# Group 3's keys and queries transposed by the DMA crossbar, through the buffer that the later groups share

## The chip, the cores and the metric

The kernel runs on one core of one Trainium2 chip. Its time is device microseconds (us) from launch to end, the median of several executions. The engines are named as in the profile: PE (TensorE, matrix multiply; PEld is its weight load, which overlaps), DVE (VectorE), ACT (ScalarE), POOL (GpSimd) and SP (SyncE). In this kernel POOL does almost nothing but issue the loads from HBM that also convert float32 to bf16. SP issues the DMA transposes and the stores of the output. SPq and POOLq are the rows of these two queues in the profile.

## What is computed

Windowed attention with a few "sink" positions, and behind it a SwiGLU block. Cut to what matters:

```python
# q, k, v: [4, 8, 768, 64] float32; n_sink = 4; window = 128
scores = (q @ k.transpose(0, 1, 3, 2)) / sqrt(64)
keep   = (pos_k < n_sink) | ((0 <= pos_q - pos_k) & (pos_q - pos_k < window))
a      = softmax(where(keep, scores, -1e9))
x      = (a @ v).transpose(0, 2, 1, 3).reshape(3072, 512)      # heads side by side

g      = x @ w_gate                                            # [3072, 1536]
out    = (g * sigmoid(g) * (x @ w_val)) @ w_out                # [3072, 512]
```

The kernel cuts the 3072 tokens into 12 attention groups of 256 tokens, three to each of the 4 batches: groups 0 to 2 belong to batch 0, groups 3 to 5 to batch 1, and so on. The SwiGLU block works in token blocks of 256, 256, 256, 512, 512, 512, 512 and 256. PE runs the SwiGLU matmuls nearly without a break, and the attention of later groups is woven in between them.

## The kernel before: the parts concerned

The scores need keys and queries with the head dimension on the partitions, but they come from HBM with the tokens there. So each group's k and q are loaded into a tile `nat` and transposed into `kT` and `qT`, 128 tokens at a time. There are two ways to do it. `step_TN` uses PE (a transpose into PSUM, then a copy by ACT or DVE). `xbar` uses DMA transposes on the SP queue, which go from on-chip memory to on-chip memory and use no compute engine.

```python
    rowp = pool("rowp", 3)
    natp = pool("natp", 1)               # one buffer
    kqtp = pool("kqtp", 2)
    ...
    def load_nat(g):
        b, c = divmod(g, GC)
        x = (natp if g > 3 else rowp).tile(
            [P, 2, 2, DM], BF16, tag="nat" if g > 3 else "rows", name="nat")
        for i, src in ((0, k), (1, q)):
            for j in range(2):           # four loads: k j0, k j1, q j0, q j1
                t0 = c * 256 + j * P
                nc.gpsimd.dma_start(
                    x[:, i, j].rearrange("p (h d) -> p h d", d=D),
                    src[b, :, t0:t0 + P].rearrange("h p d -> p h d"))
        nats[g] = x
    ...
    def step_TN(g, i, j, evict="av"):    # by PE: 4 transposes, one copy
        ...
        pt = bank([P, NP2, P], BF16, "pn")
        for p in range(NP2):
            nc.tensor.transpose(pt[:, p], nats[g][:, i, j, p * P:(p + 1) * P], ident)
        t0 = c * 256 + j * P
        dst = (kTs, qTs)[i][b][:, :, t0:t0 + P]
        if evict[i] == "a":
            nc.scalar.copy(out=dst, in_=pt)
        else:
            nc.vector.tensor_copy(out=dst, in_=pt)

    def xbar(g):                         # by DMA: k j0, q j0, k j1, q j1
        ...
        for j in range(2):
            for i in range(2):
                t0 = c * 256 + j * P
                nc.sync.dma_start_transpose(
                    (kTs, qTs)[i][b][:, :, t0:t0 + P], nats[g][:, i, j])
    ...
    def NV(g):                           # the loads of k, q and then v of a group
        return L(A(load_nat, g), A(load_v, g))
```

`step_S` computes a group's scores, in two halves of four heads. Each half needs all of the group's 256 keys and queries, and the 128 keys ahead of them if the group isn't the first of its batch. `step_K` does the scores of the sink keys. `step_PV` multiplies the weights by v, and `step_X` transposes the result into `xT` for the SwiGLU matmuls: by PE for groups 0, 1, 2 and 4, and by DMA transposes on the SP queue for the others. `gate` is one unit of the SwiGLU's first half, `down` is one of its second half, and `weave` puts attention steps into numbered units. Units 0 to 17 of the first weave are `gate`, units 18 to 23 are `down`:

```python
    ... # prologue: groups 0 and 1; POOL has issued the weights and the loads of groups 1 and 2
    load_nat(3)
    load_v(3)
    ...
    weave(us, slots(
        ...
        ((4, 4, 5, 5), TN(2)), ((6, 7), Ss(2)), (6, [K(2)]),
        ...
        (11, [NV(4)]), ((14, 14, 15, 15), TN(3, "aa")),
        (15, [A(xbar, 4)]), (15, [NV(5)]), (19, [A(xbar, 5)]), (19, [NV(6)]),
        (23, [A(xbar, 6)]), (23, [NV(7)]),
        ((17, 18), Ss(3)), (18, [A(step_ks, 1)]), (18, [A(step_vsb, 1)]),
        ((19, 19, 19, 20), PVs(3)), (20, Xs(3)),
        ((19, 20), Ss(4)), (19, [K(4)]),
        ((21, 21, 22, 22), PVs(4)), (22, Xs(4))))

    weave(gates(3) + downs(3), slots(...))   # its first unit needs all of xT of groups 3 and 4
```

The order in which the program names the steps is the order on each engine's queue. POOL issues loads one after another and waits at the first one whose buffer isn't free. SP does the same with transposes and stores. `natp` has one buffer, so a load of `nat` into it waits until the four transposes of the group before have read it. In the kernel before, group 4 is its first user.

Of the kernel before, what the change touches and what calls it, by code (L numbers as in the profile page):

```python
# [8 lines left out]
BF16 = mybir.dt.bfloat16  # L9
# [5 lines left out]
def kernel(  # L15
# [13 lines left out]
    P = 128  # L29
# [3 lines left out]
    DM = moe_w_gate.shape[0]  # L33
# [19 lines left out]
    def pool(name, bufs, psum=False):  # L53
        if psum:
            return ctx.enter_context(
                tc.tile_pool(name=name, bufs=bufs, space=bass.MemoryType.PSUM))
        return ctx.enter_context(tc.tile_pool(name=name, bufs=bufs))
# [3 lines left out]
    rowp = pool("rowp", 3)  # L61
    natp = pool("natp", 1)
# [15 lines left out]
    def bank(shape, dtype, name):  # L78
        return psum.tile(shape, dtype, tag="b", name=name)


    rows, nats, vas = {}, {}, {}
# [20 lines left out]

    def load_nat(g):
        b, c = divmod(g, GC)
        x = (natp if g > 3 else rowp).tile(
            [P, 2, 2, DM], BF16, tag="nat" if g > 3 else "rows", name="nat")
        for i, src in ((0, k), (1, q)):
            for j in range(2):
                t0 = c * 256 + j * P  # L110
# [4 lines that stand above are left out]
# [81 lines left out]
    load_gate(2)  # L196
    nc.gpsimd.tensor_copy(out=vcf[64:128], in_=vcf[0:64])
    load_nat(2)
    load_gate(3)
    load_v(2)  # L200
# [27 lines left out]
    def new_T(b):  # L228
        if b not in kTs:
            kTs[b] = kqtp.tile([P, NP2, S], BF16, tag="kT", name="kT")  # L230
            qTs[b] = kqtp.tile([P, NP2, S], BF16, tag="qT", name="qT")
# [17 lines left out]
        else:  # L249
            nc.vector.tensor_copy(out=dst, in_=pt)  # L250

    def step_TN(g, i, j, evict="av"):

        b, c = divmod(g, GC)
        new_T(b)
        pt = bank([P, NP2, P], BF16, "pn")
        for p in range(NP2):
            nc.tensor.transpose(pt[:, p], nats[g][:, i, j, p * P:(p + 1) * P], ident)  # L258
        t0 = c * 256 + j * P
        dst = (kTs, qTs)[i][b][:, :, t0:t0 + P]  # L260
        if evict[i] == "a":
            nc.scalar.copy(out=dst, in_=pt)
        else:
            nc.vector.tensor_copy(out=dst, in_=pt)
# [219 lines left out]
    def A(fn, *a):  # L484
        return lambda: fn(*a)

    def TN(g, evict="av"):
        return [A(step_TN, g, i, j, evict) for j in range(2) for i in range(2)]

    def Ss(g):  # L490
        return [A(step_S, g, p2) for p2 in range(2)]
# [108 lines left out]
    later[:0] = masks1  # L600
    flush()
    load_nat(3)
    load_v(3)

# [5 lines left out]
    def L(*fs):  # L610
        def f():
            for x in fs:
                x()
        return f

    def NV(g):
        return L(A(load_nat, g), A(load_v, g))

    weave(us, slots(
        (0, [K(1)]), (1, PVs(1)[:2] + [A(step_PV, 1, 0, 1, "a"), A(step_PV, 1, 1, 1, "a"), flush]),  # L620
        (2, [A(step_X, 1, 0, "a"), A(step_X, 1, 1, "a")]),
        ((4, 4, 5, 5), TN(2)), ((6, 7), Ss(2)), (6, [K(2)]),
        ((8, 8), PVs(2)[:2]), (9, [A(step_PV, 2, 0, 1, "a"), A(step_PV, 2, 1, 1, "a")]),
        ((10, 11), [A(step_X, 2, 0, "a"), A(step_X, 2, 1, "a")]),
        (11, [NV(4)]), ((14, 14, 15, 15), TN(3, "aa")),
        (15, [A(xbar, 4)]), (15, [NV(5)]), (19, [A(xbar, 5)]), (19, [NV(6)]),
        (23, [A(xbar, 6)]), (23, [NV(7)]),
        ((17, 18), Ss(3)), (18, [A(step_ks, 1)]), (18, [A(step_vsb, 1)]),
# [59 lines left out]
```

## Time and profile before

| what | value |
|---|---|
| time, median of 3 | 241.11 us (240.41 to 241.32) |
| span of the profiled execution | 238.4 us |
| PE busy | 229.5 us, 96% of the span, 1928 instructions |
| DVE busy | 157.8 us, 66% |
| ACT busy | 114.8 us, 48% |
| POOL busy | 73.2 us, 31% |
| DMA transposes from `nat` | 32: 16 into `kT`, 16 into `qT` |
| PE transposes from `nat` (groups 2 and 3) | 32 of 219 ns each, at 26.2 to 50.8 us |

A page of the profile lists busy time by engine, the chain of work that ended last (followed back from the last instruction, each step to what released it), and the costliest groups of instructions. The trace behind it can be asked for a timeline of one engine: start, duration, what it did, and in square brackets how long the engine had been idle and what ended that. For a DMA, the timeline shows when its engine issued it. When its data landed is given separately, as microseconds from issue to landing. A transposing DMA has no landing time of its own, so it is read from who was waiting for it.

### The profile page before, as it was taken

The numbers are of one execution on the slowest core, as the hardware profiler recorded it, in microseconds if no ns is written. First come the engines' busy times: TensorE is split into PE (matmuls) and PEld (weight loads), VectorE is DVE, ScalarE is ACT, GpSimd is POOL, SyncE is SP. The second block draws the span as 40 slices with busy tenths as digits, with TensorE's granted clock in tenths as the row PEclk, the third lists the DMA queues.
The fourth block names the chain that finished last, engine by engine and source line by source line (L and its number), as shares of the span: only waits on it lengthen the run. The fifth ranks groups of instructions, "written<-read, shape, count | busy, mean of one in ns | idle before, by whom it ended". The sixth has DMA issues, their size and how long they took to land.

```text
span 238.4 us, 4972 instructions
## 1 busy us (share of the span) xinstructions
PE 229.5 (96%) x1928; PEld 132.7 (56%) x1952; DVE 157.8 (66%) x336; ACT 114.8 (48%) x237; POOL 73.2 (31%) x94
## 2 busy tenths in 40 slices
PE   7898999999999999999999999999999999999994
PEld 4567978895554444444445454444454445488443
DVE  5698778768652898950798970688960598877000
ACT  4796485467452835512845622655622653333222
POOL 8985964703517053160171700071000000000000
PEclk9999999999999999999999999999999999999999
DMA  7999999993999979799599955799505100200122
GB/s 128 174 184 177 181 201 203 156 138 68 161 168 174 158 113 138 105 131 199 114 111 128 130 32 159 101 109 141 69 0 161 62 0 3 44 0 3 68 109 88
DMA packets 107591, 27.36 MB, mean 115 GB/s; under 512 B 94640, under 2 KB 104624, under 8 KB 107568
## 3 DMA queue, kind: packets, MB, share of 16 engines
q0 software_dynamic: 76640, 13.90, 74.1%
q1 hardware_dynamic: 30400, 12.89, 27.8%
q8 instruction: 15, 0.25, 0.4%
q10 hardware_dynamic: 528, 0.26, 0.4%
q14 instruction: 8, 0.07, 0.1%
HBM read 28.34 MB, written 6.29 MB: 145 GB/s over the span
## 4 chain that ended last, share of the span: by engine, by line
PE 85%; DMA 6%; DVE 4%; issue 2%; ACT 1%; POOL 1%; POOLq 0%; DVEq 0%; ACTq 0%
PE pd L467 26%; PE pv L436 24%; PE pg L436 24%; DMA wv<-in_moe_w_val_dram 4%; PE s L305 4%; PE o L368 4%; DMA x<-in_q_dram 2%; PE pt L243 1%; DVE u L449 1%; PE pn L258 1%; DVE xn L382 1%; DVE ht L450 1%; PE pk L333 1%; PE o L348 1%; DVE e L317 1%
## 5 line engine op out<-in xcount | busy, mean ns | idle before, releaser
L436 PE MATMUL pv<-xT,wv 128*128 128x256 bf16 (+1 forms) x376 | 73.6, 325 | 1.2 <-DMA wv<-in_moe_w_val_dram 0.5
L436 PE MATMUL pg<-xT,wg 128*128 128x256 bf16 (+1 forms) x377 | 73.5, 325 | 0.7
L443 ACT ACTIVATE th<-pg 128x512 f32<-128x512 f32 x72 | 43.4, 603 | 62.2 <-PE pg L436 58.3
L449 DVE SCALAR_TENSOR_TENSOR u<-th,pg 128x512 bf16<-128x512 f32 x72 | 49.1, 682 | 35.8 <-ACT th L443 35.8
L467 PE MATMUL pd<-wo,ht 128*128 128x512 bf16 (+1 forms) x291 | 65.0, 370 | 0.4
L450 DVE TENSOR_TENSOR ht<-u,pv 128x512 bf16<-128x512 bf16 x72 | 49.5, 687 | 11.5 <-PE pv L436 5.1
L436 PEld LDWEIGHTS <-wg 128*128 128x128 bf16 x384 | 37.4, 98 | 26.2 <-issue 0.9
L436 PEld LDWEIGHTS <-wv 128*128 128x128 bf16 x384 | 34.3, 97 | 20.4 <-issue 1.7
L312 ACT ACTIVATE e<-s 128x512 bf16<-128x512 f32 (+1 forms) x88 | 42.7, 580 | 3.9 <-PE s L305 3.9
L467 PEld LDWEIGHTS <-ht 128*128 128x128 bf16 x300 | 28.1, 98 | 28.7 <-issue 0.5
L111 POOL DMA_DIRECT2D nat<-in_k_dram x20 | 17.6, 883 | 80.2 <-DMA qT<-nat 68.2
L471 ACT ACTIVATE ot<-pd 128x512 f32<-128x512 f32 (+1 forms) x25 | 14.6, 583 | 48.4 <-PE pd L467 46.4
L317 DVE TENSOR_TENSOR e<-e,mask 128x1024 bf16<-128x1024 bf16 (+1 forms) x44 | 26.9, 648 | 3.6 <-ACT e L312 3.6
L122 POOL DMA_DIRECT2D va<-in_v_dram x24 | 21.4, 908 | 4.8 <-DMA wo<-in_moe_w_out_dram 2.5
L368 PEld LDWEIGHTS <-e 128*128 128x128 bf16 x352 | 15.4, 98 | 8.2 <-issue 0.2
L382 DVE TENSOR_TENSOR xn<-o,rcp 128x256 bf16<-128x256 f32 x44 | 18.7, 424 | 1.5
L111 POOL DMA_DIRECT2D nat<-in_q_dram x20 | 17.7, 896 | 1.2 <-DMA wv<-in_moe_w_val_dram 0.5
L368 PE MATMUL o<-va,e 128*128 128x65 bf16 x352 | 17.5, 194 | 0.2
L305 PE MATMUL s<-qT,kT 64*128 64x128 bf16 (+1 forms) x240 | 13.1, 237 | 0.0
L376 DVE RECIPROCAL rcp<-o 128x4 f32<-128x4 f32 x48 | 8.2, 174 | 5.6 <-PE o L368 5.5
L305 PEld LDWEIGHTS <-kT 64*128 64x128 bf16 x240 | 7.7, 94 | 7.3 <-issue 6.8
L133 POOL DMA_DIRECT2D wv<-in_moe_w_val_dram x6 | 4.6, 764 | 0.7 <-DMA wv<-in_moe_w_val_dram 0.5
(66 smaller groups left out, 81.6 us busy)
## 6 DMA issues: line engine op xcount, KB each, us to landing
out_dram<-ot SPq DMA_DIRECT2D x23, 256.0 KB
va<-in_v_dram POOLq DMA_DIRECT2D x24, 128.0 KB, 6.2
nat<-in_k_dram POOLq DMA_DIRECT2D x20, 128.0 KB, 3.8
nat<-in_q_dram POOLq DMA_DIRECT2D x20, 128.0 KB, 5.6
wg<-in_moe_w_gate_dram POOLq DMA_DIRECT2D x6, 256.0 KB, 7.8
wv<-in_moe_w_val_dram POOLq DMA_DIRECT2D x6, 256.0 KB, 8.4
wo<-in_moe_w_out_dram POOLq DMA_DIRECT2D x4, 384.0 KB, 11.2
st<-in_q_dram ACTq DMA_DIRECT2D x1, 256.0 KB
```

Source lines behind the costliest of these rows:

```text
L111: nc.gpsimd.dma_start(x[:, i, j].rearrange("p (h d) -> p h d", d=D), src[b, :, t0:t0 + P].rearrange("h p d -> p h d"))
L122: nc.gpsimd.dma_start(va[:, j, :, 0:D], v[b, :, t0:t0 + P].rearrange("h p d -> p h d"))
L305: nc.tensor.matmul(pss[2 * pp + h][:, col:col + n], kTs[b][r, p, kk:kk + P], qTs[b][r, p, qq:qq + n], start=True, stop=True)
L312: nc.scalar.activation(e_t[g][:, h0 + h, lo:512], pss[2 * pp + h][:, lo:512], AF.Exp, scale=scale)
L317: nc.vector.tensor_tensor(e, e, m[:, :, lo:512].broadcast_to([P, 2, 512 - lo]), op=ALU.mult)
L368: nc.tensor.matmul(o, l, r, start=(c == 0 and i == 0), stop=(i == len(mms) - 1), skip_group_check=True)
L382: nc.vector.tensor_tensor(xn, po[:, :, 0:D], rcp.broadcast_to([P, 4, D]), op=ALU.mult)
L436: nc.tensor.matmul(ps[:, i * n:(i + 1) * n], ws[fi][:, c, fo * P:(fo + 1) * P], x[:, c], start=(c == 0), stop=(c == DMC - 1))
L443: nc.scalar.activation(th, pg, AF.Tanh, scale=0.5)
L449: nc.vector.scalar_tensor_tensor(u, th, 1.0, pg, op0=ALU.add, op1=ALU.mult)
L450: nc.vector.tensor_tensor(hts[tb][:, f:f + two].rearrange("p a n -> p (a n)"), u, pv, op=ALU.mult)
L467: nc.tensor.matmul(po, hts[tb][:, f, ts * P:(ts + 1) * P], wos[f // n][:, f % n, lo:hi], start=(f == 0), stop=(f == DFC - 1))
```

## The change

Group 3 is treated like groups 4 to 11. Its `nat` comes from `natp`, and its transposes are done by the crossbar. The 16 PE transposes of group 3 and the four ACT copies behind them go. The four DMA transposes come at the head of the SP queue, ahead of group 4's. Group 4's load stays at its place in the program (unit 11), but it now finds the one buffer of `natp` in use by group 3. The change makes PE's and ACT's work shorter and leaves one way of treating these groups in the code.

```diff
     def load_nat(g):
         b, c = divmod(g, GC)
-        x = (natp if g > 3 else rowp).tile(
-            [P, 2, 2, DM], BF16, tag="nat" if g > 3 else "rows", name="nat")
+        x = (natp if g > 2 else rowp).tile(
+            [P, 2, 2, DM], BF16, tag="nat" if g > 2 else "rows", name="nat")
@@
-    def step_TN(g, i, j, evict="av"):
+    def step_TN(g, i, j):
@@
-        if evict[i] == "a":
+        if i == 0:
             nc.scalar.copy(out=dst, in_=pt)
@@
-    def TN(g, evict="av"):
-        return [A(step_TN, g, i, j, evict) for j in range(2) for i in range(2)]
+    def TN(g):
+        return [A(step_TN, g, i, j) for j in range(2) for i in range(2)]
@@
-        (11, [NV(4)]), ((14, 14, 15, 15), TN(3, "aa")),
+        (11, [A(xbar, 3)]), (11, [NV(4)]),
         (15, [A(xbar, 4)]), (15, [NV(5)]), (19, [A(xbar, 5)]), (19, [NV(6)]),
```

## The prediction

> **What bounds the kernel now.** I read the busy times first, then the chain of work that ended last, then that chain piece by piece between 45 and 80 us, and last the timelines of the two queues that feed the transposes (POOL's loads, SP's transposes). From the page:
>
> ```profile
> PE 229.5 (96%) x1928; PEld 132.7 (56%) x1952; DVE 157.8 (66%) x336; ACT 114.8 (48%) x237; POOL 73.2 (31%) x94
> ...
> PE 85%; DMA 6%; DVE 4%; issue 2%; ACT 1%; POOL 1%; POOLq 0%; DVEq 0%; ACTq 0%
> ```
>
> PE is the bound, and the DMA share of the chain is the wait for the first weights in the prologue. So whatever PE drops is gained, and whatever PE is made to wait is lost. The pieces of the chain that the change touches (start, duration, what):
>
> ```profile
> 48.36 0.45 PE pn L258 x8
> ...
> 50.56 0.45 PE pn L258 x8
> ...
> 54.50 0.44 PE s L305 x8
> ...
> 61.48 0.59 PE s L305 x12
> ...
> 76.11 0.86 PE pg L436 x4
> 76.98 0.55 PE s L305 x12
> ```
>
> The two "pn" pieces are group 3's 16 transposes. At 54.50 the scores of group 3 begin, at 61.48 those of group 4 (12 matmuls, as it isn't the first group of its batch), at 76.11 the first SwiGLU unit that needs groups 3 and 4 together, at 76.98 the scores of group 5. Now the loads, from POOL's timeline:
>
> ```profile
> 31.84 0.91 POOL L111 DMA_DIRECT2D nat<-in_k_dram  x1 [0.86 <-DMA wg<-in_moe_w_gate_dram]
> ...
> 41.42 0.88 POOL L111 DMA_DIRECT2D nat<-in_k_dram  x1 [0.59 <-DMA wo<-in_moe_w_out_dram]
> ...
> 57.64 1.75 POOL L111 DMA_DIRECT2D nat<-in_k_dram  x2 [9.56 <-DMA qT<-nat]
> ...
> 70.56 1.75 POOL L111 DMA_DIRECT2D nat<-in_k_dram  x2 [7.68 <-DMA qT<-nat]
> ...
> 86.35 1.76 POOL L111 DMA_DIRECT2D nat<-in_k_dram  x2 [10.54 <-DMA qT<-nat]
> ```
>
> These are the first loads of groups 3, 4, 5, 6 and 7. Group 4's waits for no transpose. From group 5 on each waits for the last transpose of the group before: a closed ring of load, transpose, load. The transposes, from SP's timeline:
>
> ```profile
> 49.59 1.28 SPq L272 DMA_TRANSPOSE kT<-nat  x1
> 51.39 1.84 SPq L272 DMA_TRANSPOSE qT<-nat  x1
> 53.33 1.22 SPq L272 DMA_TRANSPOSE kT<-nat  x1
> 54.64 1.23 SPq L272 DMA_TRANSPOSE qT<-nat  x1
> 59.70 0.38 SPq L472 DMA_DIRECT2D out_dram<-ot  x1
> ...
> 67.44 1.22 SPq L272 DMA_TRANSPOSE qT<-nat  x1
> 68.75 0.53 SPq L472 DMA_DIRECT2D out_dram<-ot  x1
> 69.39 2.54 SPq L401 DMA_TRANSPOSE xT<-xn  x2
> ```
>
> The first four are group 4's. The last of them is issued at 54.64, and POOL goes on at 57.64, so group 4's keys and queries are ready 61.48 − 57.64 = 3.8 us before PE wants them. That margin is what the change spends. Below it, group 3's xT stands behind group 5's transposes in the same queue.
>
> [...] the fourth bar ends at 55.87, and its waiter starts at 57.64. So I count a transpose as 3.0 us from its issue to use, not 1.2. [...] group 4's first load lands 8.1 us after 41.42, at 49.5, and the first transpose is issued at 49.59. So load, transpose and next load add up whole. [...]
>
> **What is removed.** PE loses 2 × 0.45 = 0.90 us of its chain. ACT loses four copies, two of 0.58 and two of 0.60 us in its timeline at 48.9 to 51.6. ACT stands idle for PE before the tanh units around them (0.6 to 1.15 us each), so they are off the path and worth 0. DVE's instructions stay as they are. Gain: −0.90.
>
> **What is added, step by step.**
>
> 1. Group 3's loads. Nothing ahead of them in POOL's queue changes. The landing view of the load issued at 31.84 reads:
>
> ```profile
> nat<-in_k_dram POOLq DMA_DIRECT2D x1, 128.0 KB, 12.3
> ```
>
> so the first piece is there at 44.1. By the same view the others take 11.8, 11.7 and 11.2 us from 33.38, 34.33 and 35.67, and land at 45.2, 46.0 and 46.9.
>
> 2. Group 3's transposes. SP has had nothing to do since 5 us, so they start as the pieces land, from 44.1. Group 4's in the kernel before started under the same conditions (pieces landing at 49.5 to 52.3, v loads still moving) and took from 49.59 to 57.64, 8.05 us. So group 3's are done at 52.2. PE wants them at 54.50 − 0.90 = 53.6. They are hidden, by 1.4 us.
>
> 3. Group 4's load. Its first piece goes out at 52.2 in place of 41.42, 10.8 us later. It no longer stands behind the backlog of weights, so it lands sooner after its issue.
>
> 4. Load to last transpose, with an idle DMA. Three rounds of the ring show it. Group 5: 57.64 to 70.56, 12.9. Group 9: 118.61 to 130.15, 11.5. Group 7: 86.35 to its last transpose's issue at 94.71, plus the 3.0, 11.4. I choose 12.1. Group 4 is then ready at 64.3, not 57.64.
>
> 5. PE comes to the scores of group 4 at 61.48 − 0.90 = 60.6 and stands for 3.7 us. Net so far: 3.7 − 0.90 = +2.8.
>
> 6. Group 5's round starts at 64.3, 6.7 later than before. Its transposes, one store, and group 3's two xT transposes follow in SP's order. In the kernel before the second xT is issued about 70.67 (half of the 2.54 us after 69.39), usable about 73.7 by the 3.0 of above, so 16.0 after the round's start. Now that gives 80.3. The first store then goes out before group 5's load rather than during it, and I allow 0.9 for that: 79.4 to 80.3. PE reaches that unit at 76.11 + 2.8 = 78.9. Extra wait 0.5 to 1.4, or nothing if the round is as short as group 9's. I take +0.5.
>
> 7. Later rounds. Group 6 was ready at 86.35, and its scores begin at 89.86 in PE's timeline: 3.5 of margin, against 6.7 of delay less the 3.3 that PE itself is late. Just hidden. Group 7 had been ready by 100.17 and is wanted at 113.23. From there nothing is left.
>
> Sum: −0.90 + 3.7 + 0.5 = +3.3 us. 241.1 + 3.3 = 244.4, of which I take 0.1 off for short PE gaps after 62 us that a standing PE would absorb: 244.3.
>
> **Rivals.** First, that all is hidden and only the 0.90 is seen: 240.2. For it: PE is 96% busy, and the ring has idle POOL time everywhere. Against it: the margin is 3.8 us and the delay of group 4 is 6.7. It would need a round of 8.4 us (52.2 to 60.6), and none in the trace is under 11. Second, that the wait for group 4 is paid and then the xT wait and group 6 add up: with a 12.9 round and group 3's transposes slower against the weights and v (53.5), group 4 is ready at 66.4, PE stands 5.8, and xT comes some 1 us later still: +5.9, 247.0. [...] Against it: what is left in the DMA queues after 44 us is one group's k, q and v, not two. Third, that DVE becomes the bound: it is nearly full at 80 to 100 us and follows each wait of PE. But its work isn't increased, so it moves along and adds nothing.
>
> **Range and chances.** The sum rests on three durations: 8.05 (I allow −0.7 to +1.3), 12.1 (±0.8), and the extra xT wait (0 to 1.5). That gives 1.3 to 5.2 of net loss, so 242.3 to 246.3 should hold 8 times in 10. Slower by 2% means over 245.93, a loss of 4.8, which needs the long end of two of these: 0.18. Faster by 2% would need 4.8 gained where at most 0.9 is removed: 0.01. The rest, 0.81, is within 2%.
>
> **What would show it.** Right: group 4's first load in POOL's timeline near 52, released by a transpose into qT; in the chain a DMA from nat just ahead of group 4's scores, PE idle there 3 to 5 us; group 3's scores with no wait; xT's wait small at the first unit of the next weave; POOL's rounds shifted by 6 to 7 us as far as group 7, and PE's stretch after 100 us unchanged in length. Wrong: a load of group 4 before 50 or a round under 9 us (then PE gains), PE standing at group 3's own scores (then step 2 is mis-sized), or a wait beyond group 6.

## The result, and the profile after

The changed kernel takes 244.64 us (median of 6, 244.31 to 246.01) against 241.22 us before on the same chip. The ratio is 1.0159, with a 95% interval of 1.0128 to 1.0191. (The ratios, here and below, are taken over the fast executions alone and are not the quotient of the two medians.) Measured once more beside a later experiment, it is 244.68 us, ratio 1.0132 (1.0100 to 1.0164). So the change costs about 1.5%. The prediction of 244.3 us was close, and the range held it.

The profiled execution spans 242.5 us against 238.4 before. From its page, the same two lines as before, busy time and the chain that ended last by engine, and below them the chain by line:

```profile
PE 231.7 (96%) x1936; PEld 132.4 (55%) x1936; DVE 157.9 (65%) x336; ACT 113.0 (47%) x233; POOL 73.2 (30%) x94
...
PE 73%; DMA 18%; SPq 2%; DVE 2%; POOL 2%; issue 2%; ACT 1%; POOLq 0%; DVEq 0%
PE pd L467 23%; PE pv L436 20%; PE pg L436 19%; DMA wv<-in_moe_w_val_dram 7%; DMA nat<-in_q_dram 6%; PE o L368 3%; PE s L305 3%; DMA qT<-nat 2%; SPq L272 2%; DMA xT<-xn 2%; PE w L524 2%; POOL nat L111 1%; PE pt L540 1%; PE pt L243 1%; PE o L348 1%
```

The busy shares hardly move. PE's count rises although 16 transposes are gone, because the profile before lacks 24 matmul records of the SwiGLU block (377, 376 and 291 are there, against 384, 384 and 300 after); so the two busy times can't be subtracted. The chain does move: DMA goes from 6% to 18% of it, and three names are new, group loads (`nat<-in_q`), transposes (`qT<-nat`) and `xT<-xn`. Not all of this is time in which PE stands. From 24 to 63 us the chain now runs through POOL's loads and SP's transposes, and PE works beside them most of that time (36.7 of the 39 us). PE is still busy 96% of the time, which is why the busy line alone would not have warned of it. POOL's timeline shows when the loads of groups 4, 5, 6 and 7 go out:

```profile
51.67 1.75 POOL L111 DMA_DIRECT2D nat<-in_k_dram  x2 [10.67 <-DMA qT<-nat]
...
63.97 1.76 POOL L111 DMA_DIRECT2D nat<-in_k_dram  x2 [7.04 <-DMA qT<-nat]
...
75.82 1.76 POOL L111 DMA_DIRECT2D nat<-in_k_dram  x2 [6.60 <-DMA qT<-nat]
...
91.65 1.76 POOL L111 DMA_DIRECT2D nat<-in_k_dram  x2 [10.57 <-DMA qT<-nat]
```

Group 4's load now goes out at 51.67 in place of 41.42, released by a transpose of group 3. The next three are 6.3, 5.3 and 5.3 us later than before. SP's timeline has group 3's transposes first, then group 4's, and group 3's xT behind group 5's:

```profile
44.15 1.29 SPq L272 DMA_TRANSPOSE kT<-nat  x1
46.07 1.19 SPq L272 DMA_TRANSPOSE qT<-nat  x1
47.35 1.22 SPq L272 DMA_TRANSPOSE kT<-nat  x1
48.66 1.22 SPq L272 DMA_TRANSPOSE qT<-nat  x1
55.03 1.19 SPq L272 DMA_TRANSPOSE kT<-nat  x1
...
59.75 1.22 SPq L272 DMA_TRANSPOSE qT<-nat  x1
...
74.66 2.53 SPq L401 DMA_TRANSPOSE xT<-xn  x2
```

What PE makes of it, from its timeline (the last bracket is how long it stood, and for what):

```profile
53.50 0.50 PE L305 MATMUL s<-qT,kT 64*128 64x256 bf16 x8
...
62.48 0.23 PE L305 MATMUL s<-qT,kT 64*128 64x128 bf16 x2 [1.93 <-DMA qT<-nat]
63.28 0.56 PE L305 MATMUL s<-qT,kT 64*128 64x256 bf16 x10 [0.58 <-DMA qT<-nat]
```

Group 3's scores at 53.50 wait for nothing. Group 4's begin 1.93 us late, and after two matmuls PE stands 0.58 us more, for the second half of the tokens. The chain of waits shows the second standstill:

```profile
74.70 0.66 PE pd L467 x3
75.36 0.52 SPq L401
...
75.97 3.91 DMA xT<-xn
79.88 0.14 issue
80.02 1.02 PE pg L436 x4
```

PE has run out of `down` matmuls and waits for the second xT of group 3, issued at 75.97 and usable at 79.88. The list of waits (what PE stood for, us in total, how often, the longest) has it as

```profile
PE pg L436 <- DMA xT<-xn: 2.1, 1, 2.1
```

The first `gate` unit starts at 80.02. PE's timeline of the kernel before has the same unit at

```profile
75.95 1.03 PE L436 MATMUL pg<-xT,wg 128*128 128x512 bf16 x4
```

which is 4.1 us earlier. After it nothing new is lost: the whole span is longer by 4.1 us too.

### The profile page after: what moved, and what is told of

It is laid out like the page before. It is cut to its first block, busy times and chain, and to the rows that moved or that the text cites. A ratio compares the mean times of both kernels' runs of the same rounds, so it can differ in the third digit from the quotient of the medians.

```text
span 242.5 us, 4972 instructions
## 1 busy us (share of the span) xinstructions
PE 231.7 (96%) x1936; PEld 132.4 (55%) x1936; DVE 157.9 (65%) x336; ACT 113.0 (47%) x233; POOL 73.2 (30%) x94
## 4 chain that ended last, share of the span: by engine, by line
PE 73%; DMA 18%; SPq 2%; DVE 2%; POOL 2%; issue 2%; ACT 1%; POOLq 0%; DVEq 0%
PE pd L467 23%; PE pv L436 20%; PE pg L436 19%; DMA wv<-in_moe_w_val_dram 7%; DMA nat<-in_q_dram 6%; PE o L368 3%; PE s L305 3%; DMA qT<-nat 2%; SPq L272 2%; DMA xT<-xn 2%; PE w L524 2%; POOL nat L111 1%; PE pt L540 1%; PE pt L243 1%; PE o L348 1%
## 5 line engine op out<-in xcount | busy, mean ns | idle before, releaser
L467 PE MATMUL pd<-wo,ht 128*128 128x512 bf16 (+1 forms) x300 | 66.2, 371 | 0.0
L471 ACT ACTIVATE ot<-pd 128x512 f32<-128x512 f32 (+1 forms) x25 | 14.6, 583 | 48.4 <-PE pd L467 48.4
## 6 DMA issues: line engine op xcount, KB each, us to landing
wo<-in_moe_w_out_dram POOLq DMA_DIRECT2D x4, 384.0 KB, 11.4
```

The costliest lines, as they stand in the source:

```text
L467: nc.tensor.matmul(po, hts[tb][:, f, ts * P:(ts + 1) * P], wos[f // n][:, f % n, lo:hi], start=(f == 0), stop=(f == DFC - 1))
```

## The experiments

The theory behind the prediction (A) was that the single buffer costs, by making group 4's load wait for group 3's transposes, and that the crossbar itself only takes work off PE. The rival (B) was that the four added DMA transposes cost. All ratios are to the kernel before, run on the same chip.

| kernel | median us | ratio, 95% interval |
|---|---|---|
| crossbar only, no shared buffer | 245.91 | 1.0186 (1.0155 to 1.0216) |
| shared buffer only, group 3 on PE | 244.81 | 1.0154 (1.0121 to 1.0187) |
| changed, group 3's xT by PE | 243.75 | 1.0102 (1.0069 to 1.0134) |
| changed, group 3's load ahead of the output weights | 246.08 | 1.0199 (1.0159 to 1.0240) |
| changed, shared buffer split in two | 241.02 | 1.0001 (0.9975 to 1.0027) |
| before, four added transposes that nobody reads | 242.45 | 1.0065 (1.0044 to 1.0086) |
| before, buffer split in two | 240.32 | 0.9976 (0.9960 to 0.9992) |
| changed, buffer split, first xT early | 239.98 | 0.9951 (0.9933 to 0.9969) |
| the same again | 240.23 | 0.9969 (0.9955 to 0.9983) |
| changed, again | 244.68 | 1.0132 (1.0100 to 1.0164) |

### The crossbar without the shared buffer

Against the changed kernel:

```diff
-        x = (natp if g > 2 else rowp).tile(
-            [P, 2, 2, DM], BF16, tag="nat" if g > 2 else "rows", name="nat")
+        x = (natp if g > 3 else rowp).tile(
+            [P, 2, 2, DM], BF16, tag="nat" if g > 3 else "rows", name="nat")
```

> Group 3 by the crossbar, but its load stays in the pool of three buffers, so group 4's load waits for no transpose. If the shared buffer is the cause (theory A), the added waits vanish and PE keeps the 0.90 us that it no longer spends on group 3: about 240.3 us, ratio 0.996, group 4's first load near 41.4 us, no PE wait ahead of the scores of group 4. If the four extra DMA transposes are the cause, by their place in the SP queue or by their traffic beside the weights (theory B), the loss stays: 244 us or more.

Theory A failed here. Group 4's load goes out at 41.65 as expected, and the kernel is slower, not faster: ratio 1.0186. The wait is another one. From PE's timeline of this kernel:

```profile
58.94 0.82 PE L305 MATMUL s<-qT,kT 64*128 64x256 bf16 x8 [5.07 <-DMA qT<-nat]
62.61 0.50 PE L305 MATMUL s<-qT,kT 64*128 64x256 bf16 x8
67.53 0.62 PE L305 MATMUL s<-qT,kT 64*128 64x128 bf16 x12
```

These are the scores of group 3, with 8 matmuls; group 4's, with 12, wait for nothing. PE stands 5.07 us for group 3's own transposes, and then works for 3.4 us at half its clock (see the last section). The chains show where the wait comes from. Each line is a last transpose of group 3, its issue and the time until its waiter can go on. First the changed kernel, where nothing was being loaded by then (the last load ahead of it, group 3's v, was issued at 40.12 and landed 8.3 us later, at 48.4):

```profile
48.66 2.44 DMA qT<-nat
```

and the crossbar-only kernel, where group 4's loads (issued from 41.65), and behind them group 4's own transposes (from 50.97), run beside it:

```profile
49.56 9.24 DMA qT<-nat
```

It was issued 0.9 us later and was usable 7.7 us later. This run doesn't separate the loads from the transposes beside it; the kernel that loads group 3 ahead of the output weights (below) has loads alone beside such a transpose, and shows the same (10.30 us). So the wait for the shared buffer has two sides. It makes group 4 late, and it keeps group 4's load out of the way of group 3's transposes. For the crossbar-only kernel I had still counted on the 8.05 us of a set of transposes "under the same conditions"; that set had met the end of the backlog, not its middle: it began 2.4 us after the last of the loads had gone out (49.59 against 47.2), and group 3's set here begins 3.1 us before that (45.04 against 48.1).

### The shared buffer without the crossbar

Against the kernel before:

```diff
-        x = (natp if g > 3 else rowp).tile(
-            [P, 2, 2, DM], BF16, tag="nat" if g > 3 else "rows", name="nat")
+        x = (natp if g > 2 else rowp).tile(
+            [P, 2, 2, DM], BF16, tag="nat" if g > 2 else "rows", name="nat")
```

> The complement: group 3 stays on PE as in the kernel before, but its load takes the one shared buffer. Group 4's load must then wait until PE has read group 3, at about 51 us, nearly the same moment at which the crossbar frees it (51.7). Theory A: the loss is there without any extra DMA transpose, and PE's 0.90 us of transposes lie ahead of a wait, so they cost nothing more: 244.0 to 244.9 us, ratio 1.013 to 1.016. Theory B: as the kernel before, 241.2 us.

As theory A said: 244.81 us, inside the range given, without one added DMA transpose. From POOL's timeline, and then from PE's:

```profile
51.62 1.75 POOL L111 DMA_DIRECT2D nat<-in_k_dram  x2 [10.55 <-PE pn L258]
```

```profile
62.70 0.23 PE L305 MATMUL s<-qT,kT 64*128 64x128 bf16 x2 [0.92 <-DMA qT<-nat]
63.70 0.56 PE L305 MATMUL s<-qT,kT 64*128 64x256 bf16 x10 [0.77 <-DMA qT<-nat]
```

The load goes out within 0.05 us of the changed kernel's, released by PE's transposes and not by a DMA, and group 4's scores wait in the same two steps. These waits are only 1.69 us of the loss. In this profile PE then works for 3.4 us at half its clock, which costs another 1.7, and comes to the first `gate` unit at 79.85, when xT is there. So each half of the change alone costs 1.5 to 1.9%, and both together cost no more. They aren't two costs that add. They are two ways of being late in one stretch.

### Group 3's xT by PE

Against the changed kernel:

```diff
-    PEX = (0, 1, 2, 4)
+    PEX = (0, 1, 2, 3, 4)
```

> The changed kernel with xT of group 3 made by 8 PE transposes (0.44 us by the two pieces of group 4's) in place of two DMA transposes that stand behind group 5's in the SP queue. If the second PE wait (2.1 us ahead of the first SwiGLU unit of the next weave) is a cost of its own, it goes: 244.6 - 2.1 + 0.4 = 242.9 us. If it only stands in front of the next late arrival (group 5's or group 6's scores), PE waits there and the time stays at 244 to 244.6 us.

No wait for xT is left in the list of waits, and no later group takes its place. The ratio is 1.0102 against 1.0159 and 1.0132 of the changed kernel, 0.7 to 1.4 us less where 1.7 was expected, and the intervals overlap. The part that is missing goes with a lower clock (see the last section): the two executions with a mean clock of 0.998 and 0.999 took 243.09 and 242.46 us, near the 242.9 expected, and the four with 0.992 and 0.993 took 243.44 to 244.68. So the second wait is a cost of its own, but PE's lower clock behind the first wait can use up most of what its removal gives: in this profile the first `gate` unit starts at 79.67, only 0.35 us earlier than in the changed kernel.

### Group 3's load ahead of the output weights

Against the changed kernel:

```diff
+    load_nat(3)
     for i in range(4):
         load_out(i)
 ...
-    load_nat(3)
     load_v(3)
```

> The changed kernel, with its one shared buffer, but group 3's load issued ahead of the four loads of the output weights. It lands some 6 to 7 us earlier, the ring of load, transpose and load starts near 45 us rather than 51.7, and group 4 is ready near 56 to 57, ahead of PE. Theory A (the moment at which the ring starts is what counts, not the single buffer as such): all waits vanish, 240.3 us, ratio 0.996. If one buffer is too few at any start, or if delaying the output weights costs as much: 242 us or more.

This failed too. The transposes start at 36.89, 7.3 us earlier than in the changed kernel, but run beside the output weights and group 3's v, whose loads go out up to 36.15 and 38.33. By the 11.4 us (median) and the 8.3 to 9.7 us that such loads take in the changed kernel, the last of them land at 47 to 48 us, an estimate. No other group's transposes are under way. The chain has for the last one:

```profile
41.64 10.30 DMA qT<-nat
```

It is usable at 51.94, later than the changed kernel's 51.10, and the start of the ring isn't moved forward at all (52.51 against 51.67). PE waits 1.15 + 0.96 us for group 4, less than in the changed kernel, and 3.29 us for xT, more than there. Loading earlier didn't help here: with the weights and v beside it, the last transpose took 10.30 us where it had taken 2.44.

### The shared buffer split in two

Against the changed kernel, and the same against the kernel before (there with `g > 3`):

```diff
-        x = (natp if g > 2 else rowp).tile(
-            [P, 2, 2, DM], BF16, tag="nat" if g > 2 else "rows", name="nat")
-        for i, src in ((0, k), (1, q)):
-            for j in range(2):
+        if g > 2:
+            x = [natp.tile([P, 2, DM], BF16, tag=f"nat{j}", name="nat") for j in range(2)]
+        else:
+            y = rowp.tile([P, 2, 2, DM], BF16, tag="rows", name="nat")
+            x = [y[:, j] for j in range(2)]
+        for j in range(2):
+            for i, src in ((0, k), (1, q)):
```

> The changed kernel with the shared buffer cut into two tiles of half the size, one for each 128 tokens, and the loads in the order in which the transposes want them (k j0, q j0, k j1, q j1). The memory is the same, but the first half of group 4's load waits only for the first two transposes of group 3. If the coarse wait of the ring is what costs (51.7 us to the start, 12.3 us a round), group 4's first load goes out near 48.7 us, group 4 is ready near 59.5, ahead of PE at 60.6, group 3's xT is in time, and PE keeps its 0.90 us: 240.3 us, ratio 0.996. If instead group 3's transposes are slowed by any load beside them, as in the run with the crossbar alone, PE waits at the scores of group 3 and the time is 243 us or more.

> The kernel before with the same cut of the shared buffer into two tiles and the same order of loads; group 3 stays on PE and out of the ring. No PE wait of this kernel stands behind the ring, so nothing should move: 241.0 us, ratio 0.998 to 1.002. It is there so that a gain of the split ring is not put down to the crossbar when it belongs to the split.

The loss of the changed kernel is gone: ratio 1.0001, though not the gain of 0.4% that was expected. From POOL's timeline, the first loads of groups 4 and 5, and PE's waits:

```profile
49.93 0.87 POOL L114 DMA_DIRECT2D nat<-in_k_dram  x1 [9.08 <-DMA qT<-nat]
...
61.09 0.88 POOL L114 DMA_DIRECT2D nat<-in_k_dram  x1 [5.91 <-DMA qT<-nat]
```

```profile
60.58 0.23 PE L308 MATMUL s<-qT,kT 64*128 64x128 bf16 x2 [0.16 <-DMA qT<-nat]
61.19 0.56 PE L308 MATMUL s<-qT,kT 64*128 64x256 bf16 x10 [0.37 <-DMA qT<-nat]
```

```profile
76.59 1.02 PE L439 MATMUL pg<-xT,wg 128*128 128x512 bf16 x4 [0.75 <-DMA xT<-xn]
```

Half a buffer earlier is enough for that: the ring starts 1.7 us earlier (I expected 3.0) and its first round takes 11.2 us, not 12.3. PE's waits fall from 2.5 and 2.1 us to 0.5 and 0.75. Together these are 1.3, more than the 0.90 that PE saves. The edit does two things, the cut and the new order of the loads, and no run separates them. The kernel before gains 0.24% by the same edit, which was not expected, since PE had no wait behind the ring there. Its profile doesn't show where: the first `gate` unit starts at 75.95 in both. With the edit on both sides, then, the change still costs about 0.25% (1.0001 against 0.9976), with intervals that overlap.

### Four transposes that nobody reads

Against the kernel before; `xbar_spare(3)` issues the four transposes of group 3 into a tile of its own, and group 3 stays on PE:

```diff
-        (11, [NV(4)]), ((14, 14, 15, 15), TN(3, "aa")),
+        (11, [A(xbar_spare, 3)]), (11, [NV(4)]), ((14, 14, 15, 15), TN(3, "aa")),
```

> The kernel before with four added DMA transposes of group 3's keys and queries, at the same place in the SP queue as in the changed kernel, into a tile that nobody reads. Group 3 itself stays on PE. If the added work in a stretch in which the DMA engines are full is what delays the rest, group 5's load (released by group 4's last transpose) starts near 62 us in place of 57.64, as in the run with the crossbar alone; PE hardly waits at group 4 (it comes there at 61.5) but up to 2.5 us for group 3's xT: 241.5 to 243.5 us. If only the lateness of group 3's own transposes costs, group 5's load starts near 58 us and the time is that of the kernel before.

From POOL's timeline (group 5's load), and PE's:

```profile
61.07 1.75 POOL L111 DMA_DIRECT2D nat<-in_k_dram  x2 [13.15 <-issue]
```

```profile
77.43 1.02 PE L444 MATMUL pg<-xT,wg 128*128 128x512 bf16 x4 [1.33 <-DMA xT<-xn]
```

The added transposes alone, with nobody waiting for them, put group 5's load 3.4 us later (61.07 against 57.64) and make PE wait 1.33 us for xT: 242.45 us, as the first of the two expectations had it. So rival B is a part of the truth. Crossbar work in this stretch, in which the DMA row of the kernel before shows nine tenths or more in every slice of 0.8 us from 28 to 52.8, isn't free. The loads beside it and the transposes behind it come later: group 4's first q transpose is issued 8.6 us after the q load (44.35 to 52.91) in place of 6.9 (44.45 to 51.39), and its last one at 56.21 in place of 54.64.

### A version ahead of both

The changed kernel with the split buffer, and in unit 19 of the first weave the first half of `Xs(3)` ahead of `xbar(5)`, where SP has nothing else to do (`L()` is an empty step). Against the changed kernel with the split buffer:

```diff
-        (15, [A(xbar, 4)]), (15, [NV(5)]), (19, [A(xbar, 5)]), (19, [NV(6)]),
+        (15, [A(xbar, 4)]), (15, [NV(5)]), (19, [L(), L()]),
 ...
-        ((19, 19, 19, 20), PVs(3)), (20, Xs(3)),
+        (19, PVs(3)[:2]), (19, [third]), (20, PVs(3)[3:]), (20, Xs(3)[1:]),
 ...
+    third = L(A(step_PV, 3, 0, 1), flush, A(step_X, 3, 0), flush, A(xbar, 5), NV(6))
```

> The changed kernel with the split ring, and with the first of group 3's two xT transposes put ahead of group 5's transposes in the SP queue, where SP stands idle between 59.7 and 64.4 us. The second xT then lands about 1.3 us earlier, which is more than the 0.75 us that PE still waits for it with the split ring alone. If that wait is a cost of its own: 241.0 - 0.75 = 240.3 us, ratio 0.997, and no wait for xT. If group 5 or group 6 is then the next to be late, the time stays at 241.0.

> The same kernel once more (split ring, group 3's first xT early): about 240.0 us, ratio 0.993 to 0.997, PE's wait for group 4 under 0.6 us and its wait for xT gone.

> The changed kernel once more, on the same chip as the run beside it: 244.6 us, ratio 1.013 to 1.019, PE waiting for group 4's keys and queries and for group 3's xT.

Twice, 239.98 and 240.23 us: ratios 0.9951 and 0.9969, both intervals below 1. From the second run, SP's timeline and PE's only wait for the ring:

```profile
61.61 1.20 SPq L404 DMA_TRANSPOSE xT<-xn  x1
...
72.34 1.23 SPq L404 DMA_TRANSPOSE xT<-xn  x1
```

```profile
61.55 0.56 PE L308 MATMUL s<-qT,kT 64*128 64x256 bf16 x10 [0.30 <-DMA qT<-nat]
```

The wait for xT is gone here, but not from every execution. One of the first run's 13 took 243.8 us, and its profile has

```profile
79.67 1.04 PE L439 MATMUL pg<-xT,wg 128*128 128x512 bf16 x4 [3.62 <-DMA xT<-xn]
```

Why xT came so late in that one is not known. By the ratios, this version is 0.3 to 0.5% faster than the kernel before, and so faster than both. Whether it is faster than the kernel before with the split buffer alone (0.9976) is open: the intervals overlap.

## Why the prediction was right, point by point

**Gain on PE (−0.90).** Right. Group 3's scores start at 53.50, against 54.50 (chain) or 54.43 (timeline) before, and don't wait.

**Steps 1 to 3, the start of the ring.** Right. First transpose at 44.15 (44.1 predicted), group 3 usable at 51.10 and the load out at 51.67 (52.2). Group 3's scores had 2.4 us to spare, not 1.4. The 8.05 us held (7.5, from 44.15 to 51.67) because the buffer kept group 4's loads away; in the crossbar-only kernel the set took 13.8 (45.04 to 58.80). The prediction names this condition only against its second rival (one group's loads in the queues after 44 us, "not two") and doesn't see that the buffer provides it; the crossbar-only kernel, for which I left it out and expected 240.3, came 5.6 us above that.

**Step 4, a round of 12.1.** Right for POOL: 51.67 to 63.97 is 12.3. But the 3.0 us from a transpose's issue to use was read from POOL. The chain of the changed kernel has 2.44 from issue to landing and then 0.56 on POOL itself (51.10 to 51.67). PE doesn't pay that part.

**Step 5, the wait for group 4 (3.7).** Too large: 1.93 + 0.58 = 2.5. Group 4 was usable at 63.24, not 64.3. Of the 1.06 between them, 0.73 is POOL's own part (it starts its next load at 63.97, after PE has gone on at 63.28), and the rest is the start of the ring, 0.53 earlier, less the round, 0.2 longer.

**Step 6, the extra wait for xT (0.5).** Too small: 2.1. Its arrival was right (79.4 to 80.3 predicted, 79.88 measured). What was wrong is when PE would be there, because step 5 had made PE too late. The two errors nearly cancel: xT's arrival sets the start of the next weave in any case. The prediction has this start at 78.9 + 0.5 = 79.4, and it was 80.02, 4.1 us later than before. So the loss of 3.3 us was 0.8 too small for these two profiles. That it is within 0.1 us of the difference of the medians, 3.4, is in part luck. Of these two waits, one behind the other, the last arrival was the number to get right; the first only decided how the loss is divided. The second run of the changed kernel shows this again. It stands 1.39 + 0.78 us for group 4 and 0.95 us for xT, and that `gate` unit starts at 80.46. Two of the signs named for a right prediction were therefore missed: PE idle 3 to 5 us at group 4, and a small wait for xT.

**Step 7, later groups.** Right, with more room than thought: group 6's scores start at 93.93, 2.3 us after POOL's release at 91.65, where the sum left 3.5 − (6.7 − 3.3) = 0.1. There is no wait for a transpose after 80 us, and DVE's stretch at 91 to 95 us is the one that the kernel before has at 87 to 91.

**Rivals.** "All is hidden" would have needed a round under 8.4 us; it was 12.3. "DVE becomes the bound" didn't happen. The second, with group 3's transposes slowed by loads, wasn't met in this kernel (2.44 us for the last one). Slowed transposes were met in the two experiments that let loads run beside them (9.24 and 10.30).

**Range.** The long ends of the three durations add up to 3.3 + 1.3 + 0.8 + 1.0 = 6.4 us of loss, not 5.2. The measured loss is far from either.

## What to carry to other kernels

A wait for a buffer can also be a shelter. Before taking it away, ask what the released transfer will run beside: here group 3's last transpose took 2.44 us with the loads held back, and 9.24 with group 4's loads and transposes beside it. Work moved off a full engine onto the DMA queues isn't free for that reason alone: four transposes that nobody reads cost 0.65% here. And where a ring of load, use and load sets the pace, try cutting its one buffer in two, with the loads in the order of use. Here that took the loss of 1.3 to 1.6% away for no memory, while a buffer apart for group 3, in the crossbar-only kernel, did not. A second whole buffer in `natp` was not run.

## What the hardware showed that was not expected

After PE had stood still, its granted clock fell to half for 3.4 us in some of these executions. Below are stretches of 2 us of the second run of the changed kernel. The columns are the stretch, its length, busy time and number of instructions of PE, PEld, DVE, ACT and POOL, then PE's granted clock, then two for the DMA:

```profile
60.00:62.00 2.00, 0.79 (x8) 0.22 (x5) 1.15 (x5) 0.00 (x0) 0.00 (x0) 1.00 1.82 181
...
62.00:64.00 2.00, 1.04 (x13) 0.54 (x13) 0.00 (x0) 0.45 (x1) 0.12 (x1) 1.00 0.67 196
...
64.00:66.00 2.00, 2.00 (x16) 0.85 (x16) 1.04 (x2) 2.00 (x6) 2.00 (x3) 0.59 0.24 16
...
66.00:68.00 2.00, 2.00 (x14) 0.98 (x12) 0.95 (x3) 0.28 (x1) 2.00 (x3) 0.56 1.68 107
...
68.00:70.00 2.00, 2.00 (x20) 0.88 (x18) 0.00 (x0) 0.95 (x2) 1.13 (x2) 1.00 2.14 155
```

PE stands for a good half of the first two, and in the next two it works at 0.59 and 0.56 of its clock, which costs 2 × 0.41 + 2 × 0.44 = 1.7 us. At half the clock a loss of 1.7 us takes 3.4 us, an estimate from these figures. Two stretches that lie wholly inside such a fall read 0.50: 60 to 62 us of the crossbar-only kernel and 66 to 68 of the one with the shared buffer only. The profiles of these two, of the one with xT by PE and of the one with the earlier load each have one such fall between 52 and 90 us, and the clocks of their stretches of 2 us add up to a loss of 1.70 to 1.72 us in each, again 3.4 us at half. What brings it on is not shown. It didn't take a long stretch without any work: the standstill here was only 1.39 + 0.78 us, and PE was busy for 0.79 + 1.04 of the 4 us from 60 to 64, ahead of the fall. Nor does it follow every standstill: in the first profile of the same kernel, with 1.93 + 0.58 us of standing, all four stretches from 60 to 68 us have 1.00.

One such fall lowers the mean clock of an execution to 0.993 (1.7 us of 243). By that sign (0.993 or lower) it came in 1 of 6 executions of the changed kernel at first and in all 6 later, yet the medians are 244.64 and 244.68: in the second profile the wait for xT behind the fall was 0.95 us in place of 2.1. In the kernel with xT by PE nothing was behind it to absorb it.
